# Start of a fused attention and MoE kernel: placeholder matmuls in f32, and value projections of two head pairs in one

## The chip, the cores and the metric

The kernel runs on one core of one Trainium2 chip. The metric is the device time of one execution in microseconds (us), lower is better. Times of the kernel before: 478.29, 478.55 and 478.63 us, median 478.55.

## What is computed

The reference is a Linformer attention followed by a two-layer MLP with a hard-swish between. Batch 8, 8 heads, 1024 tokens of 64 elements; E and F (64 x 1024) project the token axis of keys and values to 64.

```python
k_proj = np.einsum('ks,bhsd->bhkd', E, k)
v_proj = np.einsum('ks,bhsd->bhkd', F, v)
scores = scale * np.matmul(q, k_proj.transpose(0, 1, 3, 2))
attn = np.exp(scores - np.max(scores, axis=-1, keepdims=True))
attn = attn / (np.sum(attn, axis=-1, keepdims=True) + 1e-09)
x = np.matmul(attn, v_proj)          # then heads side by side: 8192 x 512
...
h = x @ w_in                         # 512 x 2048
g = h * np.clip(h + 3.0, 0.0, 6.0) / 6.0
return g @ w_out                     # 2048 x 512
```

All inputs and the output are f32; the kernel computes in bf16 with f32 sums.

## The kernel before

The work goes batch by batch, and each batch in two halves of 512 tokens. Heads go in pairs j = 0 to 3. The order in which each engine works is the order of the program text (`manual_schedule`): each engine runs its own instructions one after the other, and a semaphore holds an instruction until what it reads is there and what it overwrites has been read. TensorE (PE) does the matmuls; VectorE (DVE) and ScalarE (ACT) read their results from PSUM, which comes from two pools of four buffers, `pmm` (tag mm) and `pat` (tag at).

From batch 1 on, the MLP of one half runs with the attention of the next batch woven in. Batch 0 has nothing to be woven into, so its first half is a chain that starts the kernel, and the change lies all in it.

- **Lines 77 to 92.** E and F are loaded (SP and ACT queues). DVE sets the tile `ones`, and `busy(12)` (lines 87 to 92) issues twelve matmuls of 128x128 by 128x512 on it; nobody reads what `busy` writes.
- **Lines 109 to 164, POOL's queue.** In order: for each pair its k (256 KB) and its first half of q (128 KB); then the four pairs of v (256 KB each); then w_in in nine pieces; the second half of q; w_out in four pieces; then k, v, q of batch 1.
- **Lines 167 to 181.** E and F are cast, transposed on PE, and copied to `e_t` (DVE) and `f_t` (ACT, twice); then `busy(2)`.
- **`First.first_block` (lines 469 to 513).** For each pair: `keys(j)` (eight matmuls with `e_t`, DVE casts the result twice into `kp`), `sums(j - 2)`, `queries` (four transposes, a DVE copy), `scores(j - 1)` with two ACT exponentials, `keys_transposed` (two transposes, a DVE copy to `kT`). `busy(1)` stands three times in the first two pairs. After the loop come the last scores, the value projections `vals(j)` (lines 420 to 426: eight matmuls of 128x128 by 128x128 with `f_t`, then a cast of the result into `vp` on DVE, the last on ACT), the remaining `sums(j)` (two matmuls; ACT takes logarithm and exponential, which is the reciprocal `recs[j]`), and `products(j)` (two matmuls of `vp` with the weights; DVE multiplies with `recs[j]` into `xT`, line 487). Here `busy(1)` stands once more.
- **`meanwhile` and lines 622 to 632.** The first matmuls of `xT` with `w_in` (line 199, through `in_columns`, which issues each product as two of 64 columns). `meanwhile` does the first pair's share of one of them ahead of `products(3)`; from there on PE has w_in products without a break.

The order of the end of `first_block` before, which the change rewrites:

```python
scores(KO - 1)
self.vals(0, nc.vector.tensor_copy)
sums(KO - 2)
self.vals(1, nc.vector.tensor_copy)
products(0)
sums(KO - 1)
self.vals(2, nc.vector.tensor_copy)
products(1)
busy(1)
products(2)
self.vals(3, nc.scalar.copy)
meanwhile()
products(3)
```

Besides the queues that the program issues, each engine's instructions are themselves fetched by DMA (kind "instruction" in the profile; q8 carries packets of 16 KB, 50 of them in the span).

Of the kernel before, what the change touches and what calls it, by code (L numbers as in the profile page):

```python
# [8 lines left out]
f32 = mybir.dt.float32  # L9
# [6 lines left out]
def kernel(  # L16
# [11 lines left out]
    nc = tc.nc  # L28
    B, H, S, D = q.shape
# [4 lines left out]
    P = 128  # L34
    SO = S // P
    KO = d_model // P
    FO = d_ff // P
    TOK = 512
# [28 lines left out]
    def pmm():  # L67
        return ps_mm.tile([P, TOK], f32, tag="mm", name="mm")

    def pat():  # L70
        return ps_at.tile([P, TOK], f32, tag="at", name="at")


    def g_tile():
        return gpool.tile([P, FO, TOK], bf16, tag="g", name="g")

    scratch = g_tile().rearrange("p f n -> p (f n)")
    ef_f32 = scratch[:, :2 * S].bitcast(f32)
    nc.sync.dma_start(out=ef_f32[:KP], in_=E)
    nc.scalar.dma_start(out=ef_f32[KP:], in_=F)  # L80
    nc.scalar.preload_act_table_set("natural_log_exp_and_others")
    ones = consts.tile([P, TOK], bf16, name="ones")
    nc.vector.memset(ones, 1.0)
    ident = consts.tile([P, P], bf16, name="ident")


    def busy(n):
        ps = pmm()
        for _ in range(n):
            nc.tensor.matmul(ps, ones[:, :P], ones, start=True, stop=True)  # L90

    busy(12)

    def raw_tile(name):
        return kqv_pool.tile([P, H, SO, D], bf16, tag=name, name=name)


    kqv = {0: {n: raw_tile(n) for n in ("k", "q", "v")}}
# [79 lines left out]
    for a in range(2):  # L178
        nc.scalar.copy(f_t[:, :, a, :], ef_pv[:, 1])
    ef_t = [e_t, f_t[:, :, 0, :]]  # L180
    busy(2)

    def q_transposed(b):
# [212 lines left out]
    class First:  # L396
# [20 lines left out]
                                    self.kp[:, 2 * j + a].rearrange("p a d -> p (a d)"), ident[:KP, :KP])  # L417
            nc.vector.tensor_copy(self.kT[:, 2 * j:2 * j + 2, :].rearrange("p h m -> p (h m)"), ps)

        def vals(self, j, copy):  # L420
            ps = pat()[:, :P]
            for so in range(SO):
                nc.tensor.matmul(ps, f_t[:, so].rearrange("p a m -> p (a m)"),
                                 kqv[0]["v"][:, 2 * j:2 * j + 2, so, :],
                                 start=(so == 0), stop=(so == SO - 1))
            copy(self.vp[:, 2 * j:2 * j + 2, :].rearrange("p h d -> p (h d)"), ps)

        def queries(self, t, js):

# [39 lines left out]
        def first_block(self, meanwhile):  # L469
            recs = {}  # L470
            weights = spool.tile([P, FO // 2, HT], bf16, tag="sb", name="sb")

            def scores(j):
                aT = weights[:, 2 * j:2 * j + 2]
                tiles = [pmm() for _ in range(2)]
                self.scores(0, j, tiles, 0)
                for r in range(2):
                    nc.scalar.activation(aT[:, r], tiles[r][:, :HT], AF.Exp, scale=scale)
                self.aT[0, j] = aT

            def sums(j):
                recs[j] = opool.tile([P, TOK], f32, tag="o_sb", name="o_sb")
                nc.scalar.activation(recs[j], self.sums(0, j, pmm), AF.Ln)
                nc.scalar.activation(recs[j], recs[j], AF.Exp, scale=-1.0)

            def products(j):
                nc.vector.tensor_mul(self.xT[:, j, 0, :], self.values(0, j, pat), recs[j])

            for j in range(KO):
                self.keys(j)  # L490
                if j > 1:
                    sums(j - 2)
                self.queries(0, (j,))
                if j > 0:
                    scores(j - 1)
                else:
                    busy(1)
                self.keys_transposed(j)
                if j < 2:
                    busy(1)  # L500
            scores(KO - 1)
            self.vals(0, nc.vector.tensor_copy)
            sums(KO - 2)
            self.vals(1, nc.vector.tensor_copy)
            products(0)
            sums(KO - 1)
            self.vals(2, nc.vector.tensor_copy)
            products(1)
            busy(1)
            products(2)  # L510
            self.vals(3, nc.scalar.copy)
            meanwhile()
            products(3)

# [103 lines left out]
    def meanwhile():  # L618
        early.append(TwoGroups(xT, 0, g[0]))
        early[0].part(0, (0,))  # L620
# [184 lines left out]
    sums = Sums(g[1])  # L805
# [39 lines left out]
    for b in range(1, B):  # L845
# [77 lines left out]
        for t in range(NB):  # L923
            g = g_tile()
            sums = Sums(g)
            start = (b, t) == (1, 0)
# [8 lines left out]
            for what in START if start else QUADS if quads else ORDER:  # L935
                n = int(what[1:])
# [34 lines left out]
    sums = behind[0].sums  # L971
# [35 lines left out]
```

## Time and profile before

| what | value |
|---|---|
| median of three runs | 478.55 us (478.29 to 478.63) |
| the profiled execution | 478.34 us |
| its span on the core | 476.5 us |
| PE busy | 468.7 us, 6,450 matmuls and 6,450 weight loads |
| DVE, ACT, POOL busy | 340.5, 274.8, 304.7 us |
| share of the span on the chain that ended last | PE 93%, DMA 2%, ACT 2%, POOL 2% |

The span goes from the core's first recorded instruction to its last; the execution's own time is 1.8 us more. Times in the timeline are from the start of the span. A row of the timeline gives start, duration, engine, line, operation, the tile written and those read; neighbours of one kind are merged, with their number behind "x", and what an engine waited for stands in brackets. The chain that ended last is followed back from the last instruction, at each step to what released it. PEld is PE's weight load, which overlaps its matmuls.

### The profile page before, as it was taken

What the parts mean: (1) busy time and instruction counts of PE and PEld (TensorE: products, weight loads), DVE (VectorE), ACT (ScalarE), POOL (GpSimd) and SP (SyncE); (2) the same over time, 40 slices, a digit from 0 to 9 for tenths busy, and PEclk for the clock granted to TensorE, in tenths of its full rate; (3) what the DMA queues carried; (4) which work ended last, traced back from release to release, by engine and by line L of the source; (5) the groups of instructions that cost most, each with busy time, mean ns of one, the idle gap of its engine ahead of it and who ended that gap; (6) DMA issues with size and microseconds to landing.
All of it is one profiled execution on the core that took longest, in us unless ns stands there. A gap on an engine that the chain in (4) does not pass through costs nothing.

```text
span 476.5 us, 14965 instructions
## 1 busy us (share of the span) xinstructions
PE 468.7 (98%) x6450; PEld 345.4 (72%) x6450; DVE 340.5 (71%) x549; ACT 274.8 (58%) x532; POOL 304.7 (64%) x206
## 2 busy tenths in 40 slices
PE   7899999999999999999999999999999999999997
PEld 3454567567677776787787878778687877878797
DVE  3583377688765958886778876887778897747574
ACT  3666479675455654656466565666457545546451
POOL 8634956043335233867897778887778587788820
PEclk9999999999999999999999999999999999999999
DMA  9999989597997949995999197962921053111012
GB/s 167 197 201 207 240 145 205 124 164 134 243 176 137 224 114 215 200 180 132 215 160 177 48 212 154 207 130 89 214 91 45 35 151 111 45 47 45 32 60 89
DMA packets 84593, 68.65 MB, mean 144 GB/s; under 512 B 38320, under 2 KB 70576, under 8 KB 84528
## 3 DMA queue, kind: packets, MB, share of 16 engines
q0 software_dynamic: 33008, 29.36, 39.7%
q1 hardware_dynamic: 51152, 37.83, 32.3%
q8 instruction: 50, 0.82, 0.7%
q10 hardware_dynamic: 368, 0.52, 0.4%
q14 instruction: 15, 0.12, 0.1%
HBM read 71.83 MB, written 16.97 MB: 186 GB/s over the span
## 4 chain that ended last, share of the span: by engine, by line
PE 93%; DMA 2%; ACT 2%; POOL 2%; DVE 0%; issue 0%; POOLq 0%
PE mm L199 69%; PE at L199 21%; DMA v<-in_v_dram 2%; PE at L288 2%; PE at L267 1%; ACT aT L276 1%; POOL q L103 1%; POOL k L107 1%; POOL v L107 0%; PE at L457 0%; DVE parts L308 0%; ACT rec L211 0%; ACT rec L205 0%; ACT m L692 0%; PE at L437 0%
## 5 line engine op out<-in xcount | busy, mean ns | idle before, releaser
L199 PE MATMUL mm<-xT,w_in_sb 128*64 128x512 bf16 (+1 forms) x1808 | 221.4, 375 | 0.0
L563 DVE SCALAR_TENSOR_TENSOR g<-r,mm 128x512 bf16<-128x512 f32 x216 | 146.0, 681 | 71.4 <-ACT r L562 70.4
L562 ACT ACTIVATE r<-mm 128x512 f32<-128x512 f32 x216 | 128.3, 598 | 117.5 <-PE mm L199 111.4
L199 PEld LDWEIGHTS <-w_in_sb 128*64 128x64 bf16 x2048 | 117.3, 110 | 58.8 <-issue 3.0
L199 PEld LDWEIGHTS <-g 128*64 128x64 bf16 x2048 | 112.5, 110 | 24.1 <-issue 4.1
L136 POOL TENSOR_TENSOR sd<-g,sb 128x1024 bf16<-128x1024 bf16 x28 | 59.1, 2128 | 43.1 <-DVE sb L136 40.7
L133 POOL TENSOR_TENSOR sc<-g 128x2048 bf16<-128x2048 bf16 x14 | 57.0, 4073 | 44.9 <-DVE g L563 44.9
L199 PE MATMUL mm<-w_out_sb,g 128*64 128x256 bf16 (+1 forms) x1088 | 77.8, 286 | 0.0
L199 PE MATMUL at<-w_sums,g 128*64 128x256 bf16 x896 | 58.4, 273 | 0.3 <-DVE g L563 0.3
L776 POOL TENSOR_SCALAR r<-r 128x512 f32<-128x512 f32 x27 | 41.6, 1539 | 15.2 <-ACT r L771 15.2
L692 ACT COPY m<-at 128x256 f32<-128x256 f32 x84 | 31.4, 373 | 29.7 <-PE at L199 25.9
L777 POOL TENSOR_TENSOR g<-r,qm 128x512 bf16<-128x512 f32 x27 | 36.3, 1345 | 2.3
L300 DVE TENSOR_TENSOR xT<-at,rec 128x512 bf16<-128x512 f32 x54 | 34.9, 682 | 1.3 <-ACT rec L211 0.7
L136 DVE TENSOR_TENSOR o_sb<-m,mm 128x256 f32<-128x256 f32 x60 | 24.8, 413 | 9.6 <-PE mm L199 7.3
L199 PE MATMUL mm<-w_out_sb,sd 128*64 128x256 bf16 x480 | 31.3, 273 | 0.0
L199 PE MATMUL mm<-w_sums,sb 128*64 128x256 bf16 x480 | 31.2, 273 | 0.0
L276 ACT ACTIVATE aT<-at 128x512 bf16<-128x512 f32 x52 | 29.6, 601 | 2.3 <-PE at L267 2.3
L308 DVE TRANSPOSE_TENSOR_REDUCE parts<-aT 128x32 f32<-128x1024 bf16 x24 | 29.6, 1235 | 0.3 <-ACT aT L276 0.3
L199 PEld LDWEIGHTS <-sd 128*64 128x64 bf16 x480 | 26.5, 110 | 3.9 <-issue 0.2
L199 PE MATMUL at<-w_out_sb,sc 128*64 128x256 bf16 x448 | 29.3, 273 | 0.0
L199 PEld LDWEIGHTS <-sc 128*64 128x64 bf16 x480 | 26.6, 110 | 3.8 <-issue 0.3
L199 PEld LDWEIGHTS <-sb 128*64 128x64 bf16 x480 | 26.2, 110 | 4.0 <-issue 1.6
(115 smaller groups left out, 494.4 us busy)
## 6 DMA issues: line engine op xcount, KB each, us to landing
out_dram<-o_sb SPq DMA_DIRECT2D x60, 256.0 KB, 4.5
rec<-turned_rows SPq DMA_DIRECT2D x48, 256.0 KB, 6.1
k<-in_k_dram POOLq DMA_DIRECT2D x7, 1024.0 KB, 10.4
v<-in_v_dram POOLq DMA_DIRECT2D x7, 1024.0 KB, 16.1
q<-in_q_dram POOLq DMA_DIRECT2D x7, 1024.0 KB, 20.9
w_out_sb<-in_moe_w_out_dram POOLq DMA_DIRECT2D x4, 512.0 KB, 14.8
w_in_sb<-in_moe_w_in_dram POOLq DMA_DIRECT2D x7, 256.0 KB, 9.9
k<-in_k_dram POOLq DMA_DIRECT2D x4, 256.0 KB, 5.5
```

Source lines behind the costliest of these rows:

```text
L133: engine.tensor_tensor(out=out, in0=x, in1=y, op=ALU.add)
L136: engine.tensor_tensor(out=out, in0=x, in1=y, op=ALU.subtract)
L199: nc.tensor.matmul(ps[lo:lo + width], stationary[:, lo:lo + width], moving, **flags)
L276: when(lambda r=r: nc.scalar.activation(aT[:, :, r, :], tiles[r].rearrange("p (a n) -> p a n", a=2), AF.Exp, scale=scale))
L288: nc.tensor.matmul(tiles[t][c:c + D], stationary(r, 2 * j + a), self.weights(j, a)[r:r + KP], start=True, stop=True)
L300: when(lambda t=t: nc.vector.tensor_mul(self.xT[:, j, t, :], av[t], rec[:, t]))
L308: nc.vector.tensor_reduce(out=self.parts[:, j], op=ALU.add, axis=mybir.AxisListType.X, apply_transpose=True, in_=self.aT[j].rearrange("p a ...
L562: nc.scalar.activation(r, h_ps, AF.Relu, bias=0.5, scale=1.0 / 6.0)
L563: when(lambda: nc.vector.scalar_tensor_tensor(g[:, fo, :], r, 1.0, h_ps, op0=ALU.min, op1=ALU.mult))
L692: self.copy(m, ps)
L776: nc.gpsimd.tensor_scalar(out=r, in0=r, scalar1=1.0, scalar2=None, op0=ALU.min)
L777: nc.gpsimd.tensor_tensor(out=g, in0=r3, in1=h3, op=ALU.mult)
```

## The change

Two things are changed, both in batch 0.

1. `busy(n)` no longer issues n matmuls of 512 bf16 columns, but one f32 matmul for each four (or fewer) of them, over 128 columns for each: `busy(12)` is three of 512 columns, `busy(2)` one of 256, `busy(1)` one of 128. They read a part of the scratch tile that DVE now sets to 1.0 (128x1024 bf16, read as 128x512 f32), ahead of `ones`. In the built program each f32 matmul stands as two weight loads and two matmuls, so the eight f32 matmuls make 16 pairs where eighteen pairs were.
2. `vals` takes a range of pairs. Pairs 0 and 1 are projected together (eight matmuls of 256 columns where sixteen of 128 were), and their result is cast by two DVE instructions, one for each pair, as before. This stands behind `sums(KO - 2)`; then come `sums(KO - 1)`, `products(0)`, `products(1)`, and only then `vals` of pair 2. One buffer of `pat` fewer is taken.

With both, the built program has 6,440 pairs of weight load and matmul where the profile has 6,450. On DVE the memset is new, and one instruction moves: in the program before, the cast of pair 2 stands between the multiplications of `products(0)` and `products(1)`; now it stands behind both. The order on ACT, POOL and SP is the same.

```diff
     nc.scalar.preload_act_table_set("natural_log_exp_and_others")
+    nc.vector.memset(scratch[:, 3 * S:3 * S + 2 * TOK], 1.0)
     ones = consts.tile([P, TOK], bf16, name="ones")
     nc.vector.memset(ones, 1.0)
     ident = consts.tile([P, P], bf16, name="ident")
 
 
+    wide = scratch[:, 3 * S:3 * S + 2 * TOK].bitcast(f32)
+
     def busy(n):
+
         ps = pmm()
-        for _ in range(n):
-            nc.tensor.matmul(ps, ones[:, :P], ones, start=True, stop=True)
+        for lo in range(0, n, 4):
+            cols = slice(0, P * min(4, n - lo))
+            nc.tensor.matmul(ps[:, cols], wide[:, :P], wide[:, cols], start=True, stop=True)
...
-        def vals(self, j, copy):
-            ps = pat()[:, :P]
+        def vals(self, lo, hi, *copies):
+            ps = pat()[:, :(hi - lo) * P]
             for so in range(SO):
                 nc.tensor.matmul(ps, f_t[:, so].rearrange("p a m -> p (a m)"),
-                                 kqv[0]["v"][:, 2 * j:2 * j + 2, so, :],
+                                 kqv[0]["v"][:, 2 * lo:2 * hi, so, :],
                                  start=(so == 0), stop=(so == SO - 1))
-            copy(self.vp[:, 2 * j:2 * j + 2, :].rearrange("p h d -> p (h d)"), ps)
+            for j, copy in zip(range(lo, hi), copies):
+                copy(self.vp[:, 2 * j:2 * j + 2, :].rearrange("p h d -> p (h d)"), ps[:, (j - lo) * P:(j - lo + 1) * P])
...
             scores(KO - 1)
-            self.vals(0, nc.vector.tensor_copy)
             sums(KO - 2)
-            self.vals(1, nc.vector.tensor_copy)
+            self.vals(0, 2, nc.vector.tensor_copy, nc.vector.tensor_copy)
+            sums(KO - 1)
             products(0)
-            sums(KO - 1)
-            self.vals(2, nc.vector.tensor_copy)
             products(1)
+            self.vals(2, 3, nc.vector.tensor_copy)
             busy(1)
             products(2)
-            self.vals(3, nc.scalar.copy)
+            self.vals(3, 4, nc.scalar.copy)
             meanwhile()
             products(3)
```

## The prediction

> **What bounds the kernel.** First the page: engines, then the chain that ended last.
>
> ```profile
> PE 468.7 (98%) x6450; PEld 345.4 (72%) x6450; DVE 340.5 (71%) x549; ACT 274.8 (58%) x532; POOL 304.7 (64%) x206
> ...
> PE 93%; DMA 2%; ACT 2%; POOL 2%; DVE 0%; issue 0%; POOLq 0%
> PE mm L199 69%; PE at L199 21%; DMA v<-in_v_dram 2%; PE at L288 2%; PE at L267 1%; ACT aT L276 1%; POOL q L103 1%; POOL k L107 1%; POOL v L107 0%; PE at L457 0%; DVE parts L308 0%; ACT rec L211 0%; ACT rec L205 0%; ACT m L692 0%; PE at L437 0%
> ```
>
> PE is nearly always at work, and the chain runs over it, except for 2% (9.85 us) on the transfer of v at the start. Next, what PE's matmuls waited for, over the whole span:
>
> ```profile
> PE mm L457 <- ACT sb L478: 0.6, 1, 0.6
> PE at L423 <- DMA v<-in_v_dram: 0.5, 1, 0.5
> PE at L199 <- DVE g L563: 0.3, 1, 0.3
> ```
>
> Only the last of these lies behind 20 us; no matmul waits for a transfer later. So what the change does to the moment at which PE's unbroken w_in products begin (21.07) goes into the time one to one, and that moment is all that has to be worked out. The timeline of that stretch:
>
> ```profile
> 15.61 0.30 PE L450 MATMUL mm<-rec,kT 64*64 64x256 bf16 x4 [0.32 <-DVE kT L418]
> 15.77 1.19 ACT L478 ACTIVATE sb<-mm 128x256 bf16<-128x256 f32 x4
> 15.84 0.62 PE L423 MATMUL at<-v,f_t 128*128 128x128 bf16 x8
> 16.46 0.40 PE L457 MATMUL mm<-sb,ones 64*64 64x512 bf16 x2
> 16.50 0.29 DVE L426 CAST vp<-at 128x128 bf16<-128x128 f32 x1 [0.95 <-PE at L423]
> ...
> 17.35 0.40 PE L457 MATMUL at<-sb,vp 64*64 64x512 bf16 x2
> ...
> 17.86 0.69 DVE L487 TENSOR_TENSOR xT<-at,o_sb 128x512 bf16<-128x512 f32 x1
> ...
> 18.47 0.28 DVE L426 CAST vp<-at 128x128 bf16<-128x128 f32 x1
> ...
> 18.75 1.35 DVE L487 TENSOR_TENSOR xT<-at,o_sb 128x512 bf16<-128x512 f32 x2
> ...
> 19.77 0.62 PE L423 MATMUL at<-v,f_t 128*128 128x128 bf16 x8 [0.47 <-DMA v<-in_v_dram]
> ...
> 21.07 0.41 PE L199 MATMUL mm<-xT,w_in_sb 128*64 128x512 bf16 x2
> ```
>
> To be seen: the first projection (15.84) fills the 0.5 us in which PE would wait for ACT's exponentials of pair 2; the cast of pair 2 (18.47) gets between the multiplications; and the last projection (19.77) has waited 0.47 us for v. Last, that transfer. The DMA view gives 9.9 us to landing for the fourth piece of v, where the two issued in the microsecond from 8 took 6.9, and in the microsecond from 17:
>
> ```profile
> q8 instruction: 1, 0.02, 6.1%
> ```
>
> One packet of PE's instructions, 6.1% of 16 engines for 1 us, so one engine for 0.98 us. The landing marks agree: fifteen of v's sixteen parts by 18.24, the last at 19.72. The Trainium skill, "Runtime: NRT & Kernel Launch", Instruction fetch mechanics, says that an engine fetches in blocks of 16 KB, 256 instructions, at a cost mostly hidden. The packet's size agrees; hidden it is not, v being late by it. By that rule fewer PE instructions ahead of this place put the packet later, and v could land near 18.24.
>
> **The sum, part by part.**
>
> *The value projections together.* `sums` of pair 2 still starts at 16.46, since ACT's exponentials hold it; the first projection no longer fills the gap, and all of the projecting comes behind. Start of the joint projection: 16.80, as that of pair 1 now. Eight matmuls of 128 columns take PE 0.55 us to the next instruction (16.79 to 17.34), 0.056 apart; with 256 columns each is 0.053 longer, so the next one starts at 16.80 + 0.55 + 0.43 = 17.78, and the result is whole at 17.84. Two casts of 0.29, overlapping by some 0.08 as the paired casts of line 410 do: 17.88 to 18.17, and to 18.38. `sums` of pair 3, at 17.78, hides under the casts (ACT has done its exponentials at 16.96).
>
> *The products.* `products(0)` needs the first cast: 18.17 + 0.05 = 18.22. `products(1)` 0.33 later (the step from 16.46 to 16.80): 18.55. `vals` of pair 2: 18.88 to 19.50.
>
> *DVE's order.* The multiplication of a product starts 0.51 behind it (17.35 to 17.86): 18.73. The next follows 0.66 later (two in 1.35): 19.39. Only behind both comes the cast of pair 2, 0.61 later (17.86 to 18.47): 20.00 to 20.28. `products(2)` waits for it: 20.33; `vals` of pair 3, behind it on PE: 20.66. Before: 19.77. So **+0.89 us**, and v has landed by then in either case. What follows (the cast on ACT, `products(3)`, its multiplication, the w_in products) hangs on that projection as before. Queued behind the waiting `products(2)` is all of PE; behind the late cast on DVE only the multiplications of pairs 2 and 3, which are as late.
>
> Without DVE's order the cast would be free at 19.54, `products(2)` at 19.87 and the projection at 20.20, still +0.43: the gap at 16 us and the longer projection alone eat the 0.47 us that v cost.
>
> *The f32 matmuls.* Two pairs of half the column work stand for each `busy(1)`. No row has an f32 matmul; bounds from bf16 rows: each at bf16's rate (2 x 0.056 = 0.11 us), or each four times as slow (0.45), against 0.21 for the 512 columns they replace (the bf16 ones are 0.216 apart once they run fast). I take equal column work, 0.21, since the replaced time is the nearest row, plus about 0.06 for a first weight load that has nothing to hide under. By the Trainium skill, "Perfetto Trace Analysis", Engine Utilization, an f32 low/high pass has half the output rate: two passes of 128 columns at half of it are an estimated 0.21 us, the same. The first `busy(1)` ends under the wait for the cast of `kp` (8.66 to 9.12). The second and third stand right ahead of `keys`, which start as soon as PE is free (9.61, 11.30), and ACT's chain up to 16.46 starts from there: 2 x 0.06 = **+0.12**; ends -0.2 and +0.5. The fourth lies in the wait for the cast of pair 2: nothing; if DVE did not make PE wait, up to 0.3.
>
> *The start.* The new memset delays the first matmuls (1.44); the row of `ones`, 0.48 for half as many elements, bounds it by 0.96. The twelve ended at 5.49, and the transposes that follow wait for the casts of E and F until 6.71: 1.2 us of cover, so nothing. Without cover, see the third case.
>
> *Packets later on.* The other 49 instruction packets move by 20 instructions, about 1 us; no matmul waits for a transfer there: nothing, ±0.1.
>
> Sum: 0.89 + 0.12 = +1.0 us on the profiled execution's 478.34 (span 476.5 and 1.8 around it): 479.35. The median of the runs shown is 0.21 above that execution, so I give **479.5** for the median.
>
> **The cases.**
>
> 1. *Forecast*, DVE's order binds: +0.7 to +1.3, 479.2 to 479.9. Chance 0.70.
> 2. *DVE does not bind* (the casts or multiplications overlap more than the rows show): +0.2 to +0.6, 478.8 to 479.2. Against it: three instructions in program order on one engine. Chance 0.11.
> 3. *PE's clock comes late.* Before, the twelve matmuls are 0.427 apart until 4.0 us and 0.216 behind that, 2.6 us from their start; the granted clock is recorded from 4.08 on. The f32 ones start up to 0.5 later, and if each pair does not count as work enough, the fast clock may miss the transposes at 6.7. Slow, the f32 ones run 12 x 0.427 = 5.1 us, to about 7.0 (+0.35), the eight transposes (0.49) and first keys (0.45) take twice their time: +0.8 to +1.3 more, 480.2 to 481. For it: no row shows f32 at the start; against it: 0.5 us is a small delay against 1.2 of cover. Chance 0.12.
> 4. *Not slower*: v's landing is what binds, the packet moves behind it, and PE is there in time. The price of v is 0.47 us of waiting, and the gain is capped at 0.25: the first piece of w_out lands at 35.34 and PE wants it at 35.59. It decides if `products(2)` starts before 18.9, as now; by the sum above it would need 1.4 us less. The other way to it is that a later wait swallows the delay; the waits of PE beyond 20 us come to 0.3 in all. -0.25 to +0.2: 478.3 to 478.75. Chance 0.07.
>
> The range that leaves out little more than the far half of case 3 and most of case 4 is 478.75 to 480.5. A measurement of this kernel tells about 0.2%, 0.96 us, from no change; the forecast lies on that edge. Slower by more: half of case 1 (0.38), and case 3: 0.50. Faster by more than 0.2% needs four times the cap of case 4: 0.03. Within: 0.47.
>
> **What would show it.** In the profile after: `sums` of pair 2 at about 16.5 to 16.7 with PE idle ahead of it; the joint projection 0.9 to 1.0 us long; DVE's casts, two multiplications and third cast in a row from 17.9 to 20.3; the last projection at 20.6 to 20.9, waiting for no transfer; the w_in products from about 22.0; and v landing within 8.5 us instead of 9.9 if the packet has moved. I am wrong if the last projection starts before 20.2, if the w_in products start elsewhere than about 1 us late, or if the time does not follow that start.

## The result and the profile after

The changed kernel takes 480.92 us (median of seven runs, 479.12 to 480.93), the kernel before 478.34 (seven runs, 478.13 to 478.63): 2.58 us more by the medians. The ratio is 1.004, 95% interval 1.0025 to 1.0055, so slower by more than 0.2%. The median lies 0.42 above the upper end of the forecast's range; the interval of the ratio, 479.5 to 481.0 on 478.34, overlaps it.

The seven runs fall into two groups. Four took 480.92 or 480.93, with a mean granted clock of 0.996; three took 479.12, 479.41 and 479.59, with 0.999 to 1.0. The profiled execution is of the first group: 480.93, span 479.1. First its page: engines, and PE's granted clock in slices of 12 us.

```profile
PE 471.2 (98%) x6440; PEld 347.0 (72%) x6440; DVE 341.1 (71%) x550; ACT 275.0 (57%) x532; POOL 304.6 (64%) x206
...
PEclk9899999999999999999999999999999999999999
```

PE is 2.5 us longer busy with ten pairs of instructions fewer, and the second slice (12 to 24 us) shows an 8 where all was 9. The windows view resolves that slice; a row has the stretch, its length, the busy time of PE, PEld, DVE, ACT and POOL with the number of instructions, then the granted clock, the DMA share and GB/s:

```profile
13.58:17.00 3.42, 1.95 (x26) 1.14 (x23) 1.23 (x5) 2.90 (x8) 2.16 (x3) 1.00 1.25 205
17.00:20.41 3.41, 3.41 (x16) 1.42 (x15) 0.49 (x2) 2.11 (x5) 2.23 (x3) 0.50 1.56 189
20.41:23.82 3.41, 2.76 (x28) 1.62 (x28) 2.18 (x4) 1.02 (x3) 2.13 (x3) 1.00 1.45 196
```

From 17.00 to 20.41 PE ran at half its clock. In the 3.42 us before, it was busy for 1.95. In the kernel before, whose clock is recorded from 4.08 on, the stretches of the same length that hold the transposes and the same part of the work are:

```profile
4.08:7.49 3.41, 2.19 (x17) 1.09 (x15) 0.71 (x2) 0.62 (x1) 3.41 (x6) 1.00 1.23 200
...
10.90:14.32 3.42, 2.81 (x33) 1.82 (x33) 1.99 (x8) 2.38 (x6) 2.86 (x4) 1.00 1.28 203
14.32:17.73 3.41, 3.10 (x39) 1.79 (x38) 1.19 (x4) 3.06 (x8) 1.94 (x3) 1.00 1.28 207
```

The timeline of the changed kernel, against the one shown before:

```profile
16.07 0.30 PE L456 MATMUL mm<-rec,kT 64*64 64x256 bf16 x4 [0.32 <-DVE kT L423]
...
16.92 0.60 PE L463 MATMUL mm<-sb,ones 64*64 64x512 bf16 x2 [0.55 <-ACT sb L484]
...
17.45 1.89 PE L428 MATMUL at<-v,f_t 128*128 128x256 bf16 x8
...
19.37 0.49 DVE L432 CAST vp<-at 128x128 bf16<-128x128 f32 x2 [3.36 <-PE at L428]
...
20.47 1.29 DVE L493 TENSOR_TENSOR xT<-at,o_sb 128x512 bf16<-128x512 f32 x2 [0.61 <-PE at L463]
...
21.67 0.28 DVE L432 CAST vp<-at 128x128 bf16<-128x128 f32 x1
...
22.01 0.40 PE L463 MATMUL at<-sb,vp 64*64 64x512 bf16 x2 [0.63 <-DVE vp L432]
...
22.34 0.62 PE L428 MATMUL at<-v,f_t 128*128 128x128 bf16 x8
...
23.65 0.62 PE L204 MATMUL mm<-xT,w_in_sb 128*64 128x512 bf16 x4
```

The unbroken w_in products begin at 23.65 instead of 21.07: +2.58, as much as the difference of the medians. The joint projection (17.45) takes 1.81 us to the next instruction, since it runs at half the clock; the third cast (21.67) stands behind both multiplications and holds `products(2)`; the last projection waits for no transfer any more. The DMA view shows the packet of instructions in the microsecond from 18 instead of 17, and v's fourth piece back to 8.4 us from issue to landing, from 9.9:

```profile
v<-in_v_dram POOLq DMA_DIRECT2D x1, 256.0 KB, 8.4
```

By the landing marks all sixteen parts are there at 18.26, instead of 19.72. So v lands earlier, as the forecast held possible, and here it is worth nothing, for PE wants v at 22.34.

### The profile page after: what moved, and what is told of

Read it like the earlier page. It is cut to its first block, busy times and chain, and to the rows that moved or that the text cites. A ratio compares the mean times of both kernels' runs of the same rounds, so it can differ in the third digit from the quotient of the medians.

```text
span 479.1 us, 14946 instructions
## 1 busy us (share of the span) xinstructions
PE 471.2 (98%) x6440; PEld 347.0 (72%) x6440; DVE 341.1 (71%) x550; ACT 275.0 (57%) x532; POOL 304.6 (64%) x206
## 4 chain that ended last, share of the span: by engine, by line
PE 96%; ACT 3%; DVE 1%; issue 0%; DVEq 0%
PE mm L204 68%; PE at L204 20%; PE at L293 2%; PE mm L95 1%; PE at L272 1%; ACT aT L281 1%; PE at L463 1%; PE at L428 0%; PE mm L463 0%; PE at L412 0%; PE at L443 0%; ACT o_sb L490 0%; DVE parts L313 0%; ACT o_sb L489 0%; ACT sb L484 0%
```

## The experiments

The theories after the result. **G**: PE idles for 0.55 us ahead of `sums` of pair 2, because the projection of pair 0 has left that place; together with the gaps around it this makes a stretch with too little work, and the clock falls. **D**: DVE's order holds `products(2)`. **F**: the f32 placeholders delay the front. Runs of the kernel before on the same chips: median 478.13, 478.17 and 478.06 in the three sets, 477.76 to 479.05, and none of 69 with a mean clock below 0.999.

**One part at a time: f32 placeholders alone (e1), projections alone (e2).** e1 is part 1 of the change (the memset, `wide` and `busy`), e2 is part 2 (`vals` and the new order).

> Part 1 of the change alone: placeholder matmuls in f32, value projections as before. Theory F (the f32 placeholders delay the front: they run at the slow clock until about 7 us, and the second and third busy(1) each hold the following keys back by 0.1): sums of pair 2 starts 0.2 to 0.5 us later than in the kernel before (16.46), +0.2 to +0.4 in time, since v's landing takes 0.47 us of waiting out of the chain only where the packet of instructions moves behind it. Theory G (the half clock comes from PE idling once the projection of pair 0 has left the gap before sums of pair 2): that gap is filled here, so no stretch of half clock, and no run above 479.2. Rival to G (the f32 work itself makes the clock fall, because it came late or counts too little): a stretch of granted clock 0.5 here too, and runs at +1.5 or more.

Measured: 478.27 (11 runs, 477.89 to 479.09), ratio 1.0005 (0.9996 to 1.0014), no clock below 0.999. That is +0.14, less than the +0.2 to +0.4 that was expected.

```profile
16.82 0.40 PE L463 MATMUL mm<-sb,ones 64*64 64x512 bf16 x2
...
19.69 0.62 PE L429 MATMUL at<-v,f_t 128*128 128x128 bf16 x8
...
21.00 0.41 PE L205 MATMUL mm<-xT,w_in_sb 128*64 128x512 bf16 x2
```

`sums` of pair 2 is 0.36 later than before, as F says. But the packet starts at 18.04 instead of 17.69, v has landed by 18.35, the last projection does not wait, and the w_in products start 0.07 earlier than before. So in this execution the front is later, v is earlier, and the two cancel. The f32 work as such does not make the clock fall.

> Part 2 alone: projections of pairs 0 and 1 as one behind sums of pair 2, with the bf16 placeholders of before. Theory G: PE idles for 0.5 us ahead of sums of pair 2, so the clock falls in some runs or in all: those take +1.8 to +2.3 (480.2 to 480.7) with a stretch of 3.4 us at clock 0.5, the others +0.8 to +1.0 (479.1 to 479.3). Rival (f32 makes the clock fall): no half clock, all runs at +0.8 to +1.0. On DVE the third cast stands behind two multiplications either way.

Measured: 479.61 (six runs), ratio 1.0033 (1.0021 to 1.0044). Three runs have a mean clock of 0.996 and take 479.89, 479.91 and 481.05; three have 0.999 to 1.0 and take 479.27, 479.33, 479.33. So the low clock comes with part 2, and without f32. None of the three low ones lies in the 480.2 to 480.7 that was expected. The profiled execution is one without the low clock, and there DVE and PE do what the forecast had, to 0.1 us:

```profile
17.96 0.49 DVE L427 CAST vp<-at 128x128 bf16<-128x128 f32 x2 [2.33 <-PE at L423]
18.83 1.29 DVE L488 TENSOR_TENSOR xT<-at,o_sb 128x512 bf16<-128x512 f32 x2 [0.37 <-PE at L458]
20.03 0.28 DVE L427 CAST vp<-at 128x128 bf16<-128x128 f32 x1
```

```profile
16.54 0.40 PE L458 MATMUL mm<-sb,ones 64*64 64x512 bf16 x2 [0.55 <-ACT sb L479]
16.88 1.05 PE L423 MATMUL at<-v,f_t 128*128 128x256 bf16 x8
...
20.71 0.62 PE L423 MATMUL at<-v,f_t 128*128 128x128 bf16 x8
...
22.02 0.41 PE L199 MATMUL mm<-xT,w_in_sb 128*64 128x512 bf16 x2
```

From `sums` of pair 2 to the last projection it is 4.17 us, before 3.31 (16.46 to 19.77): +0.86, where the forecast had +0.89.

The gap is in this execution too (0.55 ahead of `sums` of pair 2), and the clock stays. In steps of 3.41 us from the moment at which its clock rises (5.41), the gap of pair 2 falls into another stretch than the one of pair 1 (14.25):

```profile
12.23:15.65 3.42, 2.54 (x32) 1.58 (x30) 2.03 (x8) 2.70 (x6) 2.29 (x4) 1.00 1.25 204
15.65:19.06 3.41, 2.77 (x24) 1.48 (x25) 0.72 (x3) 3.29 (x9) 2.00 (x3) 1.00 1.46 194
```

A stretch from 13.15 to 16.56, with both gaps, has 1.94 us of busy PE.

**Fill the gap (e3, e6).** The changed kernel, and part 2 alone, with unread bf16 matmuls where PE idles (three in e3, two in e6):

```diff
             scores(KO - 1)
+            fill = pat()
+            for _ in range(3):
+                nc.tensor.matmul(fill, ones[:, :P], ones, start=True, stop=True)
             sums(KO - 2)
```

> The changed kernel with three unread bf16 matmuls of 512 columns between the last scores and sums of pair 2, where PE idles. They run under ACT's exponentials, so by themselves they cost nothing. Theory G: no half clock in any run; all runs at 479.1 to 479.6, that is 1.3 to 1.8 less than the changed kernel's median of 480.92; last projection at about 20.7 to 21.1 instead of 22.34. Rival (the clock falls for another reason, the f32 work or the late start): still 480.9 in half of the runs.

> Part 2 alone (as e2_vals_only) with two unread bf16 matmuls of 512 columns in the place where PE idles. Theory G: no run with a mean clock of 0.996 (three of six in e2_vals_only had it), all at 479.0 to 479.4, which is the price of the new order alone, +0.9 to +1.0. Rival (the order itself, not the idling, makes the clock fall): as e2_vals_only, half of the runs at 479.9 to 481.

Measured: e3 479.84 (eight runs, 479.14 to 480.87), ratio 1.0034 (1.0024 to 1.0044); e6 479.13 (11 runs, 478.63 to 479.89), ratio 1.0016 (1.0008 to 1.0025). In none of the 19 runs is the mean clock below 0.999, against seven of 13 in the two kernels without the filling. So in these two kernels the fall needs the idling (in e5, below, it comes without this gap). e6 also gives the price of the new order alone: +0.96. Four of e6's eleven times lie outside the 479.0 to 479.4 that was expected (478.63 to 478.88, and 479.89). e3's times are a partial miss: only three of eight (to 479.62) lie about where expected, and its last projection starts at 21.33, not at 20.7 to 21.1. In its trace the casts of E and F start at 6.40 (before: 5.91), and the filling holds `sums` of pair 2 back by 0.13 (2.43 us behind that of pair 1, 2.30 in the changed kernel); the run of 480.87 at clock 1.0 stays unexplained.

**The gap alone (e7), and doubled (e8).** e7 is the kernel before with one line moved:

```diff
-            self.vals(0, nc.vector.tensor_copy)
             sums(KO - 2)
+            self.vals(0, nc.vector.tensor_copy)
             self.vals(1, nc.vector.tensor_copy)
```

e8 is e2 with ACT's exponentials of pair 2 done twice:

```diff
-                for r in range(2):
+                for r in [0, 1] * (2 if j == KO - 2 else 1):
                     nc.scalar.activation(aT[:, r], tiles[r][:, :HT], AF.Exp, scale=scale)
```

> The kernel before with one line moved: the projection of pair 0 behind sums of pair 2. All shapes, the placeholders, the two separate projections and DVE's order stay. Theory G: PE idles ahead of sums of pair 2, so part of the runs have a mean clock of 0.996 and take 0.6 to 1.7 more than the others. Those others: the late projection costs 0.55, the wait for v (0.47) takes most of it back: 478.1 to 478.5. Rival (the wide joint projection is needed for the clock to fall): no run at 0.996, all at 478.1 to 478.5.

> Part 2 alone (as e2_vals_only) with ACT's two exponentials of pair 2 computed twice, so that PE idles some 0.5 us longer ahead of sums of pair 2. Theory G: less work in the stretch, so the clock falls in more runs than in e2_vals_only (3 of 6), in nearly all; those at 480.4 to 481.6, any others at 479.7 to 479.9 (+0.5 on e2's 479.3). Rival (a chance of the run that does not hang on PE's idling): about half of the runs, as before.

Measured: e7 479.53 (12 runs), ratio 1.0023 (1.0014 to 1.0032). Nine runs have a mean clock of 0.996 or 0.993 and take 479.39 to 480.87, three have 0.999 or 1.0 and take 478.26 to 478.54. One moved line is enough. In its trace, ahead of the fall and behind it:

```profile
12.84:16.26 3.42, 2.00 (x26) 1.21 (x25) 1.30 (x6) 2.90 (x8) 2.24 (x3) 1.00 1.24 205
16.26:19.67 3.41, 3.41 (x27) 2.34 (x27) 0.87 (x3) 2.02 (x5) 1.48 (x2) 0.50 1.52 192
```

e8: 479.90 (five runs, 479.47 to 481.13), ratio 1.0035 (1.0023 to 1.0047). Two of five runs have a mean clock of 0.996 or 0.993, not nearly all: that expectation failed, and the length of the gap beyond the first half microsecond is not shown to raise the share of runs. In the profiled execution (mean 0.993) the clock stays low for two stretches. One run of e7 has the same mean with the gap not doubled, so it is not shown that the longer gap does this:

```profile
12.55:15.97 3.42, 2.03 (x26) 1.24 (x25) 1.40 (x6) 2.90 (x8) 2.25 (x4) 1.00 1.25 206
15.97:19.38 3.41, 2.78 (x12) 1.30 (x11) 0.28 (x2) 2.36 (x7) 1.47 (x2) 0.50 1.49 191
19.38:22.79 3.41, 3.35 (x22) 1.76 (x21) 2.00 (x6) 1.23 (x2) 3.02 (x4) 0.50 1.46 196
```

**DVE's order (e4).** The changed kernel with the projection of pair 2 ahead of `products(1)`:

```diff
             products(0)
-            products(1)
             self.vals(2, 3, nc.vector.tensor_copy)
+            products(1)
```

> The changed kernel with the projection of pair 2 ahead of products(1), so that DVE casts it between the two multiplications, as before the change. Theory D (DVE's order holds products(2)): 0.3 to 0.5 less than the changed kernel in runs of the same clock: 478.7 to 479.1 where the clock stays, 480.3 to 480.6 where it falls. Rival (PE's own order binds, not DVE's): within 0.1 of the changed kernel.

Measured: 479.93 (five runs), ratio 1.0040 (1.0027 to 1.0054); 479.21 to 479.93 at clock 1.0, 480.32 and 481.0 at 0.996. All three at clock 1.0 lie above the 478.7 to 479.1 that was expected. By times alone this is inconclusive, because the front moves by as much from run to run. The trace shows DVE's order:

```profile
18.28 0.49 DVE L432 CAST vp<-at 128x128 bf16<-128x128 f32 x2 [2.32 <-PE at L428]
19.14 0.69 DVE L493 TENSOR_TENSOR xT<-at,o_sb 128x512 bf16<-128x512 f32 x1 [0.37 <-PE at L463]
19.75 0.28 DVE L432 CAST vp<-at 128x128 bf16<-128x128 f32 x1
20.02 1.44 DVE L493 TENSOR_TENSOR xT<-at,o_sb 128x512 bf16<-128x512 f32 x2
```

The third cast is between the multiplications again, and from `sums` of pair 2 to the last projection it is 3.74 us (16.86 to 20.60), against 4.17 in e2: 0.43 for DVE's order, where the forecast had 0.46.

**Looking for a better version (e5, e9, e10).** e5 has bf16 placeholders, and pairs 0 and 1 projected together in the place of before, so that neither the gap nor DVE's order comes up; e9 is the same with two separate projections; e10 is e5 with two unread matmuls ahead of `sums` of pair 1. The diff of e5's order, against the changed kernel:

```diff
             scores(KO - 1)
+            self.vals(0, 2, nc.vector.tensor_copy, nc.vector.tensor_copy)
             sums(KO - 2)
-            self.vals(0, 2, nc.vector.tensor_copy, nc.vector.tensor_copy)
-            sums(KO - 1)
             products(0)
-            products(1)
+            sums(KO - 1)
             self.vals(2, 3, nc.vector.tensor_copy)
+            products(1)
```

> bf16 placeholders; pairs 0 and 1 projected together, but right behind the last scores, where the projection of pair 0 stood before, and with DVE's order of before: 16 PE instructions fewer ahead of v, no idling ahead of sums of pair 2, no third cast behind two multiplications. Theory: the packet of instructions falls behind v's landing (18.3 instead of 19.7), the last projection starts at about 19.1 to 19.4 instead of 19.77, no half clock: 477.6 to 478.0 against 478.13 of before (-0.1 to -0.5). Rival (the packet comes no later than before, since PE's work is as early as before): v still lands at 19.7, and the time is that of before, within 0.15. A second rival (something after v binds, w_in or w_out): v at 18.3, but the w_in products start no earlier than 20.9.

> The order of e5_joint_in_gap with the kernel before's two separate projections of pairs 0 and 1 (sixteen matmuls of 128 columns instead of eight of 256), no PE instruction fewer than before. e5 had a mean clock of 0.996 in four of eleven runs although nothing idles where the change idles. Theory W (the wide joint projection counts for less in what the clock goes by): no run at 0.996 here, 477.9 to 478.6. Rival O (the order, which leaves the ACT chain of pair 2 later, brings the low clock): three or four of eleven at 0.996, as in e5.

> e5_joint_in_gap with two unread bf16 matmuls of 512 columns ahead of sums of pair 1, in the other 0.6 us in which PE waits for ACT (13.7 to 14.3). Theory G, applied to e5: its low clock comes from the stretch that starts at about 12.4, where PE's share of streaming is least (0.41 in e5's trace, 0.39 in that of the kernel before), and the filling takes that to about 0.5: no run at 0.996, all at 477.8 to 478.7, median at that of the kernel before within 0.2. Rival (e5's low clock has another place): again a third of the runs at 479.3 to 479.7.

Measured: e5 478.50 (11 runs, 477.77 to 479.70), ratio 1.0010 (1.0001 to 1.0020); four runs at 0.996 take 479.32 to 479.70, seven 477.77 to 478.65; 477.6 to 478.0 was expected. In its trace the packet starts at 17.83, v lands at 19.84, and the last projection waits 0.49 for it: sixteen PE instructions fewer (eight matmuls and their weight loads) did not bring the packet behind v, as the rival said. e9: 478.06 (11 runs, 477.84 to 478.33), ratio 0.9998 (0.9989 to 1.0007), no low clock; e10: 478.43 (477.82 to 478.76), ratio 1.0005 (0.9995 to 1.0014), no low clock. So e5's low clock (four of eleven) was not seen without the joint projection, nor with more work in the gap of pair 1, as both W and G said; with eleven runs each, either could still be chance. Its cause is open, because no execution of e5 with a low clock was profiled, and PE's busy time does not tell e5 from the kernel before: the thinnest 3.41 us behind 7 us have 2.48 in both (12.40 to 15.81 and 12.20 to 15.61). None of the three is shown to beat the kernel before. Joining two projections saves PE next to nothing by itself: from their start to the next instruction it is 0.98 us in e5 (16.01 to 16.99) and 0.99 in e9 (16.01 to 17.00). In e9's profiled execution, with no PE instruction fewer, the packet starts at 18.06, v lands at 18.51, and the w_in products begin at 20.78, 0.29 earlier than before, after a wait of 0.39 for w_in.

## Why the prediction was right and where it was wrong

- **"What the change does to the moment at which PE's unbroken w_in products begin goes into the time one to one."** Right: +2.58 there, +2.58 in the medians. It holds in every trace: from e9 (0.29 earlier, time 0.28 less) to e8 (2.76 later, time 2.79 more), the time of the profiled execution moves as that start does, to 0.04 us.
- **The value projections together, the products, DVE's order: +0.89.** Right, where PE's clock stays at 1.0: +0.86 between the same two instructions in e2, +0.96 in time in e6; of it 0.43 by DVE's order (forecast 0.46).
- **v's landing.** Right in what came of it: the packet no longer delays v (8.4 us instead of 9.9), and there was no gain, since `products(2)` started at 20.37 in e2 where case 4 needed 18.9. e1, where PE is there in time, shows the gain that can be had: it paid back 0.36 us of delay. The reason given, fewer PE instructions ahead, is not shown: e5 has sixteen fewer and a late v (19.84), e9 none fewer and an early one (18.51).
- **The f32 matmuls: +0.12.** Too low, but inside the bounds. `keys` of pair 1 starts 0.36 later than before (9.97 for 9.61) and that of pair 2 0.45 later (11.75 for 11.30), where the first `keys` is 0.27 later (8.18 for 7.91): 0.09 for each of the two `busy(1)`, so 0.18. The equal column work that the forecast took is not what the trace has: the second of the two f32 matmuls starts 0.21 behind the first (9.55, 9.76), and the next instruction another 0.21 behind that, near the slow bound of 0.45 for both. That the net came out close is luck, for the bf16 one, too, took longer than the 0.21 put down for it: 0.33 to the next instruction.
- **"The start ... nothing."** Mis-sized. In the profiled execution the casts of E and F start 0.31 later (6.22 for 5.91), and the first `keys` 0.27 later. That is probably not the change, for the casts wait for the transfers of E and F: over the twelve traces they start anywhere from 5.24 to 6.40, and the ranges of the two kinds of placeholders overlap (bf16 5.24 to 6.18, f32 5.74 to 6.40). In e1 they start at 5.74, 0.17 earlier than before, and the first `keys` is still 0.17 later (8.09): there the f32 matmuls hold the transposes, for some 0.3 us. They are 0.85 apart at 512 columns, and the granted clock is recorded only from 6.56 on. So the cover of 1.2 us was not enough in e1.
- **Case 3, "PE's clock comes late".** The late clock is real, but f32 is not shown to be its reason: the clock rises at 6.76 in the changed kernel and at 4.08 in the one before, but at 5.41 in e2 and at 7.41 in e5, both with bf16 placeholders. It differs from trace to trace. That 480.92 lies in this case's 480.2 to 481 is luck: what made it is another low clock, ten microseconds later.
- **The step that failed** is one the prediction did not have: of the gap ahead of `sums` of pair 2 it counted that work moved out of it, not that PE's idling itself could cost. In four of seven runs the clock falls to a half behind it, for 3.41 us. Its price in the profiled execution: 5.42 us from `sums` of pair 2 to the last projection (16.92 to 22.34), against 4.17 in e2: +1.25. Front +0.46 (16.92 for 16.46), order +0.86 and clock +1.25 make the 2.57 by which the last projection is later (22.34 for 19.77). The sum closes because the clock's share is what e2's order leaves; by times, the low runs of the changed kernel take 1.3 to 1.8 more than its others.
- **The number.** 479.5 was the case without the fall; the three runs without it took 479.12 to 479.59. With four runs of seven in the other group, it is partly chance that the median is 480.92 and not near 479.5. By the prediction's own signs of being wrong, the profiled execution counts against it: its w_in products start 2.58 us late, not about 1.

How the clock goes: it rises, falls and rises again at 6.76, 17.00 and 20.41 in the changed kernel, and 17.00 is three steps of 3.413 behind 6.76. In e7 it falls at 16.26, three such steps behind its rise at 6.02. So in these traces the clock changes on a grid of 3.41 us whose start differs from trace to trace. A fall then needs a stretch of the grid that holds most of the idle time of both gaps, which would explain why some runs have it and others not; the profiled executions of e2 and e4, where the grid parts the gaps (at 15.65 and 16.13), agree. The stretches ahead of a fall had 1.95, 2.00 and 2.03 us of busy PE (changed kernel, e7, e8); the thinnest in the traces that was followed by full clock had 2.19 (kernel before, 4.08 to 7.49). The Trainium skill, "TensorE: Matmul & The Clock Gate", Part 1, has this grid (a free-running window of 3413 ns) and the half rate; the traces agree with both. The Trainium skill, "TensorE: Matmul & The Clock Gate", "Why this matters for your kernels", advises to leave PE idle for no more than about 3 us between bursts of matmuls. Here the longest single gap in the stretch ahead of the fall was 0.61 us (ahead of `sums` of pair 1), so keeping to that advice was not enough. Where exactly the bound lies, and whether PE's busy time is what is counted, the runs leave open; e5 speaks against busy time alone.

## What to carry to other kernels

Work that stands in an engine's wait can be worth more than its own time. With PE's half microsecond left idle in a thin part of the program, the clock fell in four of seven runs, at a price of 1.25 us in the profiled one; so before moving PE work out of a gap, add up PE's busy time over every 3.4 us around it. When a cast moves behind other work on its engine, follow who waits for the cast: 0.43 us here. And a transfer that lands earlier is worth something only where the engine that reads it would have waited for it.

## What the runs showed that was not expected

- PE's clock fell to 0.5 for 3.41 us behind a stretch with 57% of busy PE (1.95 of 3.42). In e8 it stayed at 0.5 for 6.82, though PE was busy for 2.78 of the first 3.41 of them.
- Where a packet of 16 KB of PE's instructions came early, the last of v's sixteen parts landed 1.48 us behind the others (19.72 for 18.24, kernel before). Packets at 17.46 to 17.69 went with a late v (19.48 to 19.72; e8, e6, e7, before), packets at 18.04 and later with one by 18.51 (e1, e9, the changed kernel). In between it went both ways: at 17.80 v landed at 18.26 (e2), at 17.83 at 19.84 (e5). In e10 the packet came at 16.17 and v at 18.91.
- An f32 `busy(1)` of 128 columns holds PE for 0.42 us to the next instruction (9.55 to 9.97 in the changed kernel), a bf16 one of 512 columns for 0.33 (9.28 to 9.61 in the kernel before).
